# One reciprocal for a head's four chunks, and the norm's mean and epsilon inside the logarithm, in an attention kernel with two mixer blocks

## The chip, the cores and the metric

One core of a Trainium2 chip runs the kernel. The metric is device time in microseconds (us) of one execution. A profiled execution gives, beside its time, the time of every instruction on the engines: PE (TensorE: matmuls and transposes, PEld being its weight loads), DVE (VectorE), ACT (ScalarE), POOL (GpSimd) and SP (SyncE, whose queue issues the DMAs).

## The reference

Attention over 4 batches of 12 heads (448 tokens, 64 wide), with q and k normalized by their root mean square, and then two mixers over tokens and channels:

```python
def _attn_ref(q, k, v, g_q, g_k):
    def rmsnorm(x, g):
        rms = np.sqrt(np.mean(x * x, axis=-1, keepdims=True) + 1e-06)
        return x / rms * g
    q_n, k_n = (rmsnorm(q, g_q), rmsnorm(k, g_k))
    scores = (1.0 / np.sqrt(q.shape[-1])) * np.matmul(q_n, k_n.transpose(0, 1, 3, 2))
    scores = scores - np.max(scores, axis=-1, keepdims=True)
    attn = np.exp(scores)
    attn = attn / (np.sum(attn, axis=-1, keepdims=True) + 1e-09)
    return np.matmul(attn, v)
# x: (4, 448, 768) from the heads; h = ((x^T U) V)^T; u = x + h
# x = u + relu(u @ w_ch1) @ w_ch2                      w_ch1: 768 x 3072
# u = x + (relu(x^T @ w_tok1) @ w_tok2)^T
# out = u + relu(u @ w_ch1') @ w_ch2'                  w_ch1': 768 x 1536
```

## The kernel before

**Stages.** The heads are numbered 0 to 47; two neighbours make a pair, and a pair's q, k and v are loaded together. Heads 0 to 23 (batches 0 and 1) run alone at the start: the lone heads. The number 24 at which this ends is called `seam`. Heads 24 to 47 (batches 2 and 3) run beside the first mixer's channel product of batches 0 and 1 (`ffn`). Everything behind that is mixers: their weights come as 64 bit words, are converted on ACT, DVE and POOL (`to_f32`, tiles `w_bits`, lines 130 to 139), and are split in two parts each.

**A pair's norm** is `load_pair`: squares (`sq`, line 378) and their sums (`ms`, line 379), then on 16 columns the mean with epsilon (line 381), an ACT logarithm and an ACT exponential of minus half of it (lines 383, 384), and a Newton step (`nt`, lines 386 to 389) that gives the factor `rs`; q and k times `rs` are `qn` and `kn` (line 397). For pair 0 the small operations run on DVE (`first`), for all others on POOL. `turn_pair` transposes q and k on PE (`tt`), splits them in `both`, and lays them out by DMA in `qs` and `ks`.

**A head's softmax** is `softmax`: four chunks of 112 rows, and for each a score product on PE (`sc`), a negated row maximum on DVE (`nm`, line 459) and an exponential on ACT (`p`, line 461), which also leaves the row's sum in a column of `sm`. After every second chunk POOL adds 1e-9 to the two sums (line 464), DVE takes their reciprocal (line 465) and POOL scales the two chunks (line 468). A lone head's softmax stands two heads ahead of its product with v, `weigh`: transposes of the four chunks on PE (`pt`), copies on ACT and DVE (`ph`, `pl`), and products (`pv`). For the lone heads `p` has 12 buffers, three heads' worth, and the scores have three PSUM banks.

**Order.** Program text order isn't what the engines run: the framework places each engine's instructions by a simulated timeline when the program is built. Each engine then runs its own list in order, waiting at semaphores. So an edit in one place can reorder the lists elsewhere.

Of the kernel before, what the change touches and what calls it, by code (L numbers as in the profile page):

```python
# [9 lines left out]
F32 = mybir.dt.float32  # L10
# [3 lines left out]
AF = mybir.ActivationFunctionType  # L14
ALU = mybir.AluOpType
# [9 lines left out]
def attention_then_two_mixers(  # L25
# [30 lines left out]
    nc = tc.nc  # L56
    P = 128
    B, H, S, D = q.shape
    DM = out.shape[2]
    CP, NC4 = 112, 4  # L60
# [9 lines left out]
    const = ctx.enter_context(tc.tile_pool(name="const", bufs=1))  # L70
# [21 lines left out]
    for o in (0, D):  # L92
        nc.scalar.dma_start(gq2[o:o + D], g_q.rearrange("(d o) -> d o", o=1))
        nc.scalar.dma_start(gk2[o:o + D], g_k.rearrange("(d o) -> d o", o=1))
    gg = const.tile([P, 1], F32, name="gg")
    nc.vector.tensor_mul(gg, gq2, gk2)
    nc.vector.tensor_scalar_mul(gg, gg, 1.0 / D ** 0.5)
# [7 lines left out]
    pools = {"late": False, "split_u": nc.vector}  # L105
# [7 lines left out]
    def psum(kind, shape, name):  # L113
        pool = pools[kind]
        return pool.tile(shape, F32, tag=pool.name, name=name)
# [241 lines left out]
    def fetch_heads(b, hp, names):  # L357

        h0 = 2 * hp
        res = []  # L360
        for nm in names:
            t = pools["at"].tile([CP, 2, NC4, D], F32, tag="vr" if nm == "v" else "qkr", bufs=AT[nm + "r"],
                        name=f"{nm}r")
            nc.sync.dma_start(t, dict(q=q, k=k, v=v)[nm][b, h0:h0 + 2].rearrange(
                "h (p c) d -> p h c d", c=NC4))
            res.append(t)
        return res

    def load_pair(b, hp, turn, qk):
        first = turn == 0  # L370
        mul = nc.vector.tensor_mul if turn in (0, 2, 3) else nc.gpsimd.tensor_mul
        qr, kr, vr = qk + fetch_heads(b, hp, "v")

        ms = pools["at"].tile([CP, 2, 8], F32, tag="ms", name="ms")
        for i, t in enumerate((qr, kr)):
            sq = pools["at"].tile([CP, 2 * NC4, D], F32, tag="sq", bufs=AT["sq"], name="sq")
            tt = t.rearrange("p h c d -> p (h c) d")
            mul(sq, tt, tt)
            nc.vector.reduce_sum(ms[:, i], sq, axis=AX.X)
        small = nc.vector if first else nc.gpsimd  # L380
        small.tensor_scalar(ms, ms, 1.0 / D, 1e-6, op0=ALU.mult, op1=ALU.add)
        rs = pools["at"].tile([CP, 2, 8], F32, tag="rs", name="rs")
        nc.scalar.activation(rs, ms, AF.Ln)
        nc.scalar.activation(rs, rs, AF.Exp, scale=-0.5)
        nt = pools["at"].tile([CP, 2, 8], F32, tag="nt", name="nt")
        small.tensor_mul(nt, rs, rs)
        small.tensor_mul(nt, nt, ms)
        small.tensor_scalar(nt, nt, -0.5, 1.5, op0=ALU.mult, op1=ALU.add)
        small.tensor_mul(rs, rs, nt)

        def scale(i, shape):
            return rs[:, i].rearrange("p (h c) -> p h c", h=2).unsqueeze(3).to_broadcast(shape)

        qn, kn = [], []
        for i, (nm, t, n) in enumerate((("qn", qr, qn), ("kn", kr, kn))):
            n.append(pools["at"].tile([CP, NC4, 2, D], F32, tag=nm, bufs=AT["qn"], name=nm))
            mul(
                n[0].rearrange("p c h d -> p h c d"), t, scale(i, [CP, 2, NC4, D]))
        qn, kn = qn[0], kn[0]

        return qn, kn, vr
# [45 lines left out]
            res.append((qs, ks[:, 0], ks[:, 1]))  # L447
        return res

    def softmax(pr, qs, ks, kt):  # L450
        for c in range(NC4):
            if c % 2 == 0:
                sm = pools["at"].tile([CP, 2], F32, tag="sm", bufs=6, name="sm")
            sc = psum("s", [CP, S], "sc")
            cs = slice(c * CP, (c + 1) * CP)
            mm(sc, qs[:, cs], ks, True, False)
            mm(sc, qs[:, cs], kt, False, True)
            nm = pools["at"].tile([CP, 1], F32, tag="nm", bufs=8, name="nm")
            nc.vector.tensor_reduce(nm, sc, axis=AX.X, op=ALU.max, negate=True)  # L459
            p = pools["pp"].tile([CP, S], F32, tag="p", bufs=AT["p"], name="p")  # L460
            nc.scalar.activation(p, sc, AF.Exp, bias=nm, accum_out=sm[:, c % 2:c % 2 + 1])  # L461
            pr.append(p)
            if c % 2:
                nc.gpsimd.tensor_scalar_add(sm, sm, 1e-9)
                nc.vector.reciprocal(sm, sm)  # L465
                for i in range(2):
                    x = pr[c - 1 + i]
                    nc.gpsimd.tensor_scalar(x, x, sm[:, i:i + 1], 1.0, op0=ALU.mult, op1=ALU.mult)  # L468
            yield

# [42 lines left out]
    def attention(pairs, seam):  # L513
# [3 lines left out]
        n = 2 * len(pairs)  # L517
        loaded, turned, values, probs, fetched = {}, {}, {}, {}, {}
        dst = None

        def soft(h):
            if not 0 <= h < n:
                return iter(())
            probs[h] = []
            return softmax(probs[h], *turned[h // 2][h % 2])

        for t in range(-8, n):
            ahead = 2 if t < seam else 1
# [20 lines left out]
            h = due(3)  # L549
# [3 lines left out]
            h = due(7)  # L553
            if h < n:
                fetched[h // 2] = fetch_heads(*pairs[h // 2][:2], "qk")
            h = due(5)
# [632 lines left out]
```

## Time and profile before

| | |
|---|---|
| median of 3 runs | 1529.53 us (1521.19, 1529.53, 1531.46) |
| profiled execution, its own time | 1526.91 us |
| its span, first to last instruction | 1525.1 us |
| mean granted clock of TensorE | 0.985 |
| busy share of the span: PE, DVE, POOL, ACT | 94%, 77%, 59%, 49% |

The span is 1.8 us shorter than the execution's time. The busy shares are means over stages that differ much: POOL is at 59% over the whole, but at over nine tenths in parts of the first 200 us. A time in the rows below is counted from the first instruction of the span.

### The profile page before, as it was taken

What the parts mean: (1) busy time and instruction counts of PE and PEld (TensorE: products, weight loads), DVE (VectorE), ACT (ScalarE), POOL (GpSimd) and SP (SyncE); (2) the same over time, 40 slices, a digit from 0 to 9 for tenths busy, and PEclk for the clock granted to TensorE, in tenths of its full rate; (3) what the DMA queues carried; (4) which work ended last, traced back from release to release, by engine and by line L of the source; (5) the groups of instructions that cost most, each with busy time, mean ns of one, the idle gap of its engine ahead of it and who ended that gap; (6) DMA issues with size and microseconds to landing.
All of it is one profiled execution on the core that took longest, in us unless ns stands there. A gap on an engine that the chain in (4) does not pass through costs nothing.

```text
span 1525.1 us, 22086 instructions
## 1 busy us (share of the span) xinstructions
PE 1436.3 (94%) x7396; PEld 1271.5 (83%) x7396; DVE 1170.3 (77%) x1805; ACT 745.6 (49%) x1508; POOL 902.3 (59%) x943
## 2 busy tenths in 40 slices
PE   4899988999999999999999999999999999989997
PEld 3666767888888889888898998888999998979996
DVE  6888877888787788676758675477898988577886
ACT  4687755666566665444535343335343431334421
POOL 5889936777766565455655454047777755213842
PEclk9999979999999999999999999999999999999999
DMA  6676646777766565765637664355445463323343
GB/s 170 151 174 153 151 163 208 245 212 224 236 209 199 166 209 188 247 231 189 221 120 248 227 238 143 102 194 154 157 148 163 147 196 118 120 83 120 126 123 103
DMA packets 144385, 266.06 MB, mean 174 GB/s; under 512 B 12832, under 2 KB 104448, under 8 KB 144160
## 3 DMA queue, kind: packets, MB, share of 16 engines
q1 hardware_dynamic: 143952, 264.65, 55.6%
q8 instruction: 59, 0.97, 0.3%
q14 instruction: 54, 0.44, 0.1%
q10 hardware_dynamic: 320, 0.00, 0.0%
HBM read 149.72 MB, written 79.10 MB: 150 GB/s over the span
## 4 chain that ended last, share of the span: by engine, by line
PE 52%; DVE 8%; DMA 4%; POOL 3%; ACT 2%; issue 2%; SPq 0%; DVEq 0%; POOLq 0%; ACTq 0%
PE ps_x L79 23%; PE ps_p L79 10%; PE ps_g L79 10%; PE ps_t L79 2%; PE ps_u L79 2%; DVE w_bits L136 1%; DVE w_bits L131 1%; DVE w_bits L132 1%; POOL w L150 1%; PE pv L79 1%; ACT w_bits L130 1%; PE pt L487 1%; PE sc L79 1%; POOL w_bits L139 1%; DMA qs<-both 1%
## 5 line engine op out<-in xcount | busy, mean ns | idle before, releaser
L79 PE MATMUL ps_x<-gs,w 128*128 128x448 f32 x1440 | 326.0, 373 | 7.6 <-DVE gs L656 3.9
L79 PE MATMUL ps_g<-u,w 128*128 128x448 f32 x1440 | 312.7, 370 | 4.0 <-DMA w<-h_a 1.6
L79 PEld LDWEIGHTS ps_x<-gs,w 128*128 128x128 f32 x1440 | 267.9, 191 | 34.5 <-DVE gs L656 6.9
L79 PEld LDWEIGHTS ps_g<-u,w 128*128 128x128 f32 x1440 | 270.2, 189 | 27.6 <-DMA w<-h_a 1.8
L79 PE MATMUL ps_x<-gs,w_b 128*128 128x448 f32 x1026 | 226.5, 366 | 6.9 <-DVE xT L852 3.9
L139 POOL TENSOR_TENSOR w_bits<-w_bits,w_round 128x768 uint32<-128x768 uint32 (+3 forms) x80 | 145.1, 1814 | 121.0 <-DVE w_bits L136 68.9
L79 PEld LDWEIGHTS ps_x<-gs,w_b 128*128 128x128 f32 x1026 | 191.9, 188 | 24.4 <-DVE xT L852 5.0
L150 POOL TENSOR_TENSOR w<-w_bits,w 128x768 fp32r<-128x768 f32 (+3 forms) x82 | 148.1, 1816 | 82.9 <-ACT w L149 74.8
L686 DVE TENSOR_TENSOR xT<-ps_x,xT 128x448 f32<-128x448 f32 x216 | 132.2, 618 | 43.5 <-PE ps_x L79 41.2
L150 POOL TENSOR_TENSOR w_b<-w_f,w_b 128x384 fp32r<-128x384 f32 x104 | 119.0, 1157 | 68.2 <-ACT w_b L149 67.9
L468 POOL TENSOR_SCALAR p<-p,sm 112x448 f32<-112x448 f32 x192 | 131.4, 697 | 19.4 <-DVE sm L465 16.1
L79 PE MATMUL sc<-ks,qs 128*112 128x448 f32 x384 | 125.2, 412 | 18.5 <-ACT p L461 15.2
L461 ACT ACTIVATE p<-sc,nm 112x448 f32<-112x448 f32 x192 | 121.5, 635 | 37.8 <-DVE nm L459 36.4
L300 POOL TENSOR_TENSOR w_f<-w_f 128x384 f32<-128x384 f32 x26 | 29.1, 1118 | 176.1 <-DMA w_f<-c_a 99.0
L459 DVE TENSOR_REDUCE nm<-sc 112x1 f32<-112x448 f32 x192 | 116.0, 614 | 12.4 <-PE sc L79 11.9
L487 PEld LDWEIGHTS pt<-ident,p 112*112 112x112 f32 x768 | 88.6, 134 | 32.2 <-issue 9.1
L487 PE MATMUL pt<-ident,p 112*112 112x112 f32 x768 | 109.3, 260 | 3.0 <-DVE pl L502 1.9
L498 ACT ACTIVATE ph<-pt 112x448 fp32r<-112x448 f32 (+1 forms) x168 | 88.3, 545 | 38.4 <-PE pt L487 37.5
L131 DVE TENSOR_SCALAR w_bits<-w_bits 128x768 f32<-128x768 f32 (+3 forms) x80 | 65.2, 815 | 52.4 <-ACT w_bits L130 52.3
L135 ACT ACTIVATE w_round<-w_raw 128x768 uint32<-128x768 uint32 (+3 forms) x80 | 69.9, 874 | 66.4 <-POOL w_bits L139 60.0
L502 DVE TENSOR_TENSOR pl<-pt,ph 112x448 fp32r<-112x448 f32 x144 | 86.9, 615 | 18.3 <-ACT ph L498 17.8
L130 ACT ACTIVATE w_bits<-w_raw 128x768 f32<-128x768 f32 (+3 forms) x80 | 70.0, 875 | 57.5 <-POOL w L150 31.1
(141 smaller groups left out, 2718.0 us busy)
## 6 DMA issues: line engine op xcount, KB each, us to landing
w_raw<-in_moe_w_ch_dram SPq DMA_DIRECT2D x72, 768.0 KB, 5.1
w_b<-h_a SPq DMA_DIRECT2D x65, 384.0 KB, 4.3
h_a<-w SPq DMA_DIRECT2D x56, 384.0 KB, 2.7
ks<-both SPq DMA_DIRECT2D x92, 224.0 KB, 3.7
c_a<-w_bits SPq DMA_DIRECT2D x40, 384.0 KB, 4.4
w_f<-c_a SPq DMA_DIRECT2D x40, 384.0 KB, 3.1
h_b<-w SPq DMA_DIRECT2D x32, 384.0 KB, 2.5
w_b<-h_b SPq DMA_DIRECT2D x29, 384.0 KB, 3.8
```

What stands on the lines that cost most here:

```text
L79: nc.tensor.matmul(o, lhsT=l, rhs=r, start=start, stop=stop)
L130: nc.scalar.activation(f(w), f(high), AF.Abs)
L131: nc.vector.tensor_scalar_max(f(w), f(w), TINY)
L139: nc.gpsimd.tensor_tensor(w, w, r, op=ALU.add)
L150: nc.gpsimd.tensor_sub(lo, w, f(hi))
L459: nc.vector.tensor_reduce(nm, sc, axis=AX.X, op=ALU.max, negate=True)
L461: nc.scalar.activation(p, sc, AF.Exp, bias=nm, accum_out=sm[:, c % 2:c % 2 + 1])
L468: nc.gpsimd.tensor_scalar(x, x, sm[:, i:i + 1], 1.0, op0=ALU.mult, op1=ALU.mult)
L487: nc.tensor.transpose(pt[:, c * CP:(c + 1) * CP], pr[c][:, kc * CP:(kc + 1) * CP], ident[:CP, :CP],)
L498: nc.scalar.activation(ph, pt, AF.Copy)
L502: nc.vector.tensor_sub(pl, pt, f(ph))
L686: nc.vector.tensor_add(xT[:, dc], px, xT[:, dc])
```

## The change

Lone heads from the third on (`2 <= h < seam`, 22 heads) take all four sums in one tile of four columns: one addition of 1e-9, one reciprocal and then four scalings, where there were two additions, two reciprocals and twice two scalings. Heads 0, 1 and 24 to 47 keep groups of two. The tile `sm` has 4 buffers of four columns in place of 6 of two.

In the norm, the logarithm now reads the raw sum of squares, with the scale 1/64 and the epsilon as its bias from a new constant tile `eps`. The Newton step's other factor, minus half of the mean with epsilon, is one operation into `nt` that needs only `ms`, and stands beside the logarithm and not ahead of it. The square of `rs` goes into `ms`. For pair 0, on DVE, the last two operations become one. For the other pairs POOL has as many operations as before, five.

```diff
+    eps = const.tile([P, 1], F32, name="eps")
+    nc.vector.memset(eps, 1e-6)
...
         small = nc.vector if first else nc.gpsimd
-        small.tensor_scalar(ms, ms, 1.0 / D, 1e-6, op0=ALU.mult, op1=ALU.add)
+        nt = pools["at"].tile([CP, 2, 8], F32, tag="nt", name="nt")
         rs = pools["at"].tile([CP, 2, 8], F32, tag="rs", name="rs")
-        nc.scalar.activation(rs, ms, AF.Ln)
+        nc.scalar.activation(rs, ms, AF.Ln, scale=1.0 / D, bias=eps[:CP])
+        small.tensor_scalar(nt, ms, -0.5 / D, -0.5e-6, op0=ALU.mult, op1=ALU.add)
         nc.scalar.activation(rs, rs, AF.Exp, scale=-0.5)
-        nt = pools["at"].tile([CP, 2, 8], F32, tag="nt", name="nt")
-        small.tensor_mul(nt, rs, rs)
+        small.tensor_mul(ms, rs, rs)
         small.tensor_mul(nt, nt, ms)
-        small.tensor_scalar(nt, nt, -0.5, 1.5, op0=ALU.mult, op1=ALU.add)
-        small.tensor_mul(rs, rs, nt)
+        if first:
+            small.scalar_tensor_tensor(rs, nt, 1.5, rs, op0=ALU.add, op1=ALU.mult)
+        else:
+            small.tensor_scalar_add(nt, nt, 1.5)
+            small.tensor_mul(rs, rs, nt)
...
-    def softmax(pr, qs, ks, kt):
+    def softmax(pr, n, qs, ks, kt):
         for c in range(NC4):
-            if c % 2 == 0:
-                sm = pools["at"].tile([CP, 2], F32, tag="sm", bufs=6, name="sm")
+            if c % n == 0:
+                sm = pools["at"].tile([CP, NC4], F32, tag="sm", bufs=4, name="sm")[:, :n]
...
-            nc.scalar.activation(p, sc, AF.Exp, bias=nm, accum_out=sm[:, c % 2:c % 2 + 1])
+            nc.scalar.activation(p, sc, AF.Exp, bias=nm, accum_out=sm[:, c % n:c % n + 1])
             pr.append(p)
-            if c % 2:
+            if c % n == n - 1:
                 nc.gpsimd.tensor_scalar_add(sm, sm, 1e-9)
                 nc.vector.reciprocal(sm, sm)
-                for i in range(2):
-                    x = pr[c - 1 + i]
+                for i in range(n):
+                    x = pr[c + 1 - n + i]
                     nc.gpsimd.tensor_scalar(x, x, sm[:, i:i + 1], 1.0, op0=ALU.mult, op1=ALU.mult)
...
-            return softmax(probs[h], *turned[h // 2][h % 2])
+            return softmax(probs[h], NC4 if 2 <= h < seam else 2, *turned[h // 2][h % 2])
```

Where this puts the instructions: over the program DVE has 22 fewer, POOL 22 fewer, and PE, ACT and SP as many as before. Lines of the changed kernel count 2 more from the norm on and 5 more behind it (the scaling is its line 473, the addition 469). Each engine's list is in another order up to the end of the attention; behind that it is the same list.

On POOL, before, from the scaling of head 17 to that of head 18, among the later lone heads (`vs` is the split of v, `sq` the squares of a later pair):

```order
L468 TENSOR_SCALAR p<-p,sm 112x448 x2
L464 TENSOR_SCALAR sm<-sm 112x2
L386 TENSOR_TENSOR nt<-rs 112x16
L468 TENSOR_SCALAR p<-p,sm 112x448 x2
L150 TENSOR_TENSOR vs<-vr,vs 112x4x64
L387 TENSOR_TENSOR nt<-nt,ms 112x16
L464 TENSOR_SCALAR sm<-sm 112x2
L378 TENSOR_TENSOR sq<-kr 112x512
L468 TENSOR_SCALAR p<-p,sm 112x448 x2
L388 TENSOR_SCALAR nt<-nt 112x16
L464 TENSOR_SCALAR sm<-sm 112x2
L468 TENSOR_SCALAR p<-p,sm 112x448 x2
```

On POOL, in the changed kernel, the scaling of head 18 with what stands ahead of it:

```order
L469 TENSOR_SCALAR sm<-sm 112x4
L152 TENSOR_TENSOR vs<-vr,vs 112x4x64
L386 TENSOR_SCALAR nt<-ms 112x16
L380 TENSOR_TENSOR sq<-qr 112x512
L394 TENSOR_TENSOR rs<-rs,nt 112x16
L473 TENSOR_SCALAR p<-p,sm 112x448 x4
```

One addition of four columns stands where there were two of two, with four other operations between it and the four scalings, which now stand in one run.

On DVE, before, the norm of pair 0 at the start of the program:

```order
L381 TENSOR_SCALAR ms<-ms 112x16
L96 TENSOR_TENSOR gg<-gq_72,gk_73 128x1
L97 TENSOR_SCALAR gg<-gg 128x1
L386 TENSOR_TENSOR nt<-rs 112x16
L387 TENSOR_TENSOR nt<-nt,ms 112x16
L388 TENSOR_SCALAR nt<-nt 112x16
L379 TENSOR_REDUCE ms<-sq 112x8
L389 TENSOR_TENSOR rs<-rs,nt 112x16
L397 TENSOR_TENSOR qn<-qr,rs 112x2x4x64
```

On DVE, in the changed kernel, the same place:

```order
L386 TENSOR_SCALAR nt<-ms 112x16
L98 TENSOR_TENSOR gg<-gq_72,gk_73 128x1
L99 TENSOR_SCALAR gg<-gg 128x1
L388 TENSOR_TENSOR ms<-rs 112x16
L389 TENSOR_TENSOR nt<-nt,ms 112x16
L391 SCALAR_TENSOR_TENSOR rs<-nt,rs 112x16
L381 TENSOR_REDUCE ms<-sq 112x8
L402 TENSOR_TENSOR qn<-qr,rs 112x2x4x64
```

The product of the two gains (`gg`, which waits for their DMAs) still stands ahead of the Newton step; the factor `rs` is ready one operation and one reduction earlier in the list, and the scaling of q keeps its place behind the reduction.

## Rows read from the trace of the kernel before

**Rows 1.** The page of the whole execution: span, and each engine's busy us.

```profile
span 1525.1 us, 22086 instructions
...
PE 1436.3 (94%) x7396; PEld 1271.5 (83%) x7396; DVE 1170.3 (77%) x1805; ACT 745.6 (49%) x1508; POOL 902.3 (59%) x943
```

**Rows 2.** Busy us of each engine in stretches; PEclk is the granted clock.

```profile
core 0: us, PE busy (x) PEld busy (x) DVE busy (x) ACT busy (x) POOL busy (x), PEclk, DMA share, GB/s
...
45.00:100.00 55.00, 49.66 (x284) 37.46 (x283) 46.27 (x97) 40.06 (x111) 45.74 (x87) 0.97 0.63 152
100.00:133.00 33.00, 28.46 (x158) 19.95 (x157) 30.86 (x64) 25.12 (x68) 30.97 (x55) 1.00 0.65 160
133.00:188.00 55.00, 53.15 (x317) 39.79 (x316) 47.47 (x99) 43.94 (x119) 51.68 (x99) 1.00 0.64 157
...
196.00:240.00 44.00, 36.64 (x154) 29.26 (x154) 35.10 (x59) 26.10 (x48) 16.75 (x12) 0.81 0.50 169
240.00:300.00 60.00, 54.22 (x286) 47.40 (x286) 47.08 (x83) 35.53 (x77) 46.46 (x53) 0.97 0.74 225
```

**Rows 3.** Lines of POOL's additions (L464), from 45, 100 and 133 us on.

```profile
L464 POOL TENSOR_SCALAR sm<-sm 112x2 f32<-112x2 f32 x15 | 3.2, 214 | 4.3 <-ACT p L461 3.3
...
L464 POOL TENSOR_SCALAR sm<-sm 112x2 f32<-112x2 f32 x10 | 2.1, 214 | 0.9
...
L464 POOL TENSOR_SCALAR sm<-sm 112x2 f32<-112x2 f32 x16 | 3.4, 214 | 1.4
```

**Rows 4.** Timeline of POOL, 172 to 176 us.

```profile
172.06 0.21 POOL L464 TENSOR_SCALAR sm<-sm 112x2 f32<-112x2 f32 x1
172.35 0.20 POOL L381 TENSOR_SCALAR ms<-ms 112x16 f32<-112x16 f32 x1
...
175.01 0.21 POOL L464 TENSOR_SCALAR sm<-sm 112x2 f32<-112x2 f32 x1
175.32 1.26 POOL L468 TENSOR_SCALAR p<-p,sm 112x448 f32<-112x448 f32 x2
```

**Rows 5.** Timeline: end of head 13's last exponential (ACT), its first scaling (POOL).

```profile
115.45 0.24 ACT L461 ACTIVATION_READ_ACCUMULATOR p<-sc,nm 112x1 f32 x1
...
122.83 1.26 POOL L468 TENSOR_SCALAR p<-p,sm 112x448 f32<-112x448 f32 x2
```

**Rows 6.** Timeline of PE, 122 to 124 us.

```profile
122.15 0.91 PE L79 MATMUL pv<-ph,vr 112*128 112x448 f32 x2
122.55 0.71 PE L79 MATMUL pv<-pl,vs 112*128 112x448 f32 x1
123.10 0.55 PE L487 MATMUL pt<-ident,p 112*112 112x112 f32 x4
123.42 0.64 PE L79 MATMUL sc<-ks,qs 128*112 128x448 f32 x2
```

**Rows 7.** Timeline of the start: norms of pairs 0 and 2.

```profile
8.22 0.17 DVE L387 TENSOR_TENSOR nt<-nt,ms 112x16 f32<-112x16 f32 x1
8.43 0.17 DVE L388 TENSOR_SCALAR nt<-nt 112x16 f32<-112x16 f32 x1
...
17.39 0.69 DVE L379 TENSOR_REDUCE ms<-sq 112x8 f32<-112x512 f32 x1
...
18.24 0.20 POOL L381 TENSOR_SCALAR ms<-ms 112x16 f32<-112x16 f32 x1
```

**Rows 8.** Lines of ACT and DVE, 100 to 196 us.

```profile
L465 DVE RECIPROCAL sm<-sm 112x2 f32<-112x2 f32 x26 | 4.0, 156 | 1.3 <-POOL sm L464 1.1
L429 ACT ACTIVATE both<-tt 128x448 fp32r<-128x448 f32 x7 | 3.9, 559 | 0.6 <-PE tt L418 0.4 <-DMA ks<-both 0.2
L425 ACT ACTIVATE both<-tt,gg 128x448 fp32r<-128x448 f32 x6 | 3.8, 637 | 3.6 <-issue 1.6 <-DMA ks<-both 1.1 <-DMA qs<-both 0.9
```

**Rows 9.** Waits from 200 to 615 us: engine, waited for, total, times, longest.

```profile
POOL sm L464 <- ACT p L461: 32.0, 26, 4.6
...
PE sc L79 <- ACT p L461: 8.5, 7, 2.4
```

## The prediction

> **What bounds the kernel now.** I read the page first, then the time by stretches, then in the stretch that the change touches the lines of POOL and its timeline, and last the waits.
>
> The page gives PE 1436.3 us of a span of 1525.1 [rows 1], so over the whole program PE is the engine that is hardly ever without work. The change removes nothing from PE. It can pay only where PE waits, and only in the first 200 us, since that is where lone heads run. The stretches show how much there is to win [rows 2] (the columns are the stretch, its length, then the busy time of PE, PEld, DVE, ACT and POOL). From 45 to 100 us PE is busy 49.66 of 55, so it idles 5.3; from 100 to 133 it idles 4.5; from 133 to 188 only 1.85. POOL idles 9.3, 2.0 and 3.3 there. DVE is nearly as full, 30.86 of 33 in the second stretch. The lone heads thus have no engine that is alone the bound. POOL and DVE are the tightest in the second stretch, PE in the third.
>
> That PE's 1.85 us are real in the third kind of stretch is to be read from starts, since matmuls overlap: at 122.15 a product, at 122.55 the next, at 123.10 four transposes, at 123.42 score products [rows 6]. Each starts before the one ahead has ended. PE is handed work there as fast as it takes it.
>
> A rule speaks against this reading. The Trainium skill ("Perfetto Trace Analysis", section "Identifying the Most-Contended Engine") holds matmul busy time to be a poor measure of how full TensorE is, because pipelined matmuls mislead, and would have weight-load busy time used. Weight loads are busy 39.79 of the 55 us [rows 2], so by that page PE would have 15 us to spare and the whole of POOL's saving would come through; the time it gives is a rival below.
>
> POOL's place is seen in one head. The last of head 13's four exponentials is done at 115.69 (115.45 and 0.24), and POOL comes to the head's first scaling at 122.83 [rows 5]: 7.1 us later, with its own list in between. A scaling waits for POOL's list, not for exponentials.
>
> **The change part by part.**
>
> The removed additions on POOL. An addition at 172.06 is followed by POOL's next operation at 172.35, one at 175.01 by the next at 175.32 [rows 4]: 0.30 each, nearly all of it fixed. The trace has no addition of four columns; an operation of POOL on 16 columns takes 0.20, as long as one on two (0.21) [rows 4], so I take the same 0.30. Half of the additions in each stretch go [rows 3].
> - 45 to 100 us: 15 additions, 7.5 of them go, 2.2 us. POOL idles 9.3 here, 4.3 of it right ahead of additions, 3.3 for exponentials [rows 2, 3], so some of the saving becomes idle time. I take half, 1.1; the bounds are 0 and 2.2.
> - 100 to 133 us: 10, so 5 go, 1.5 us. POOL is full, and PE has 4.5 us to take it up. I take 1.5.
> - 133 to 188 us: 16, so 8 go, 2.4 us. PE can gain no more than its 1.85 us of idle time. I take half of that, 0.9; the bounds are 0 and 2.4, the upper if PE isn't full after all.
>
> Sum 3.5 us. The first 45 us hold only the first few heads, two of which keep their groups, and the pipeline is filling there; I take nothing.
>
> The removed reciprocals on DVE: 22 of 0.156 [rows 8], 3.4 us. They lie beside other work, except that in the second stretch DVE is as full as POOL; that the 1.5 us above come through there needs this relief too. I count no more for it. If it hid nothing, the saving on POOL in that stretch would stop at DVE's 2.1 idle us, which is still over 1.5.
>
> The added wait. The first two chunks' scalings now wait for the fourth exponential. What covers this is the 7.1 us that POOL is late [rows 5], and that POOL idles only 0.9 and 1.4 us ahead of its additions in the two later stretches, none of it listed as a wait for ACT [rows 3]. I take 0. If the cover were gone, the whole list of POOL behind the addition would wait: scalings of the head before, the norm, `qn` and `kn`, and with them PE's `tt`. That is a rival.
>
> The norm. For pair 0 one operation of DVE goes: 8.22 to 8.43, 0.21 [rows 7]. The start of the logarithm comes earlier by as much, but the Newton step stands behind `gg` in DVE's list as before. For the other pairs a hop over POOL goes from the path: pair 2's sums end on DVE at 18.08 (17.39 and 0.69), and POOL starts the mean only at 18.24 and ends it at 18.44 [rows 7], 0.36 that ACT need not wait. While the pipeline fills this is on the path, later `load_pair` is pairs ahead of its use. I take 0.5 for both, with bounds 0 and 1.
>
> ACT's logarithm gets its bias from a tile. The nearest rows: the copy with a scale from a tile (`gg`) takes 637 ns, the one without 559 [rows 8], so 0.08 each, 2 us for 24, half of it in the lone stage. ACT is busy 43.94 of 55 where it is fullest [rows 2], so this hides; 0, at worst 1. The Trainium skill ("ScalarE: Activation LUTs", section "What ACT_TABLE_LOAD costs") puts each such operand at about 93 ns, an estimate of 2.2 us for 24 by its figure; the trace agrees within 0.02 each, and the sum stays as it is.
>
> The order from 196 us to the end of the attention. Nothing is removed there, but every list is permuted locally. I take 0, with a width from what waits there: PE idles 7.4 us from 196 to 240 (at a granted clock of 0.81, so between 1.2 and 2.4 GHz) and 5.8 to 300 [rows 2], 13 us that a better order could win at most; it waits 8.5 us in 7 pieces for a score bank [rows 9], and as much again is what I give a worse one. Behind the attention the lists are the same, so what was won or lost is passed on.
>
> Sum: 3.5 + 0.5 = 4.0 us. Against the profiled execution, 1526.9 - 4.0 = 1522.9. That execution lies 2.6 below the median of three; the mean of all four is 1527.3, and from it I forecast 1527.3 - 4.0 = **1523.3 us**. A measurement of this kernel can tell about 1% from no change, 15 us: under 1512 is faster, over 1542.6 slower.
>
> **The rivals.**
> - *PE was the bound in the lone stage.* POOL's and DVE's freed time becomes idle time. For it: PE's unbroken starts [rows 6]. Against it: 9.8 us of idle PE from 45 to 133. Time: 1527.3.
> - *POOL alone sets the pace.* All bounds at once, 2.2 + 1.5 + 2.4 + 1.0 = 7.1: 1520.2. For it: POOL's 7 us of lateness. This is what the page on weight loads would have, and the starts in [rows 6] speak against it in the longest stretch.
> - *The addition stalls POOL* (slower). If POOL comes to a lone head's addition before the fourth exponential is done, its list stands. Beside the mixer this is so already: 26 waits, 32.0 us, 1.23 each [rows 9]. At that price 22 heads cost 27 us: 1523.3 + 27 = 1550. It decides where POOL's lateness falls under the time of two exponentials; a saving of 0.3 a head doesn't use up 7 us.
> - *A new order beside the mixer.* Well placed, 13 us more: 1510.3. Badly, 8.5: 1531.8.
>
> **How the numbers follow.** Forecast 0.40, PE the bound 0.22, POOL alone 0.12, stalls of POOL 0.08, a better order 0.10, a worse one 0.08. The last two have no better ground than that local moves of up to some tens of matmuls can fall either way. Faster by over 1% is the better order, 0.10; slower is the stalls, 0.08; the rest, 0.82, is within 1%. The range goes from about the better order's end, 1511, to past the worse one's, 1537, where the runs' own spread of some 5 us to either side is added; it leaves out the stalls and half of the better order.
>
> **What would show it.** In the changed kernel POOL should have 74 additions, no more idle time ahead of those of the lone heads than now, and the lone stage's last heads should end some 4 us earlier, PE's idle time from 45 to 188 us being smaller by about that. Waits of POOL for exponentials in the lone stage would show the stall; an unmoved end of the stage would show PE as the bound; a stage that ends earlier and a mixer that doesn't would show the order. The forecast fails if the second stage moves by more than the first can give.

## The result, and the profile after

The changed kernel takes **1537.71 us** (median of 10 runs, 1534.92 to 1541.00), the kernel before 1528.74 (10 runs, 1521.19 to 1533.47). The ratio of the two, taken over their runs, is 1.0072, with a 95% interval of 1.0049 to 1.0095: slower by 9 us going by the medians, by 11 going by the ratio. The forecast was 1523.3, its range ended at 1537. The change went the other way than forecast. A worse order was among the rivals, but it was looked for in the wrong place, beside the mixer.

The page of the changed kernel, span and busy us of each engine (`...` marks lines left out, here and below):

```profile
span 1534.2 us, 22056 instructions
...
PE 1444.4 (94%) x7396; PEld 1273.9 (83%) x7396; DVE 1177.9 (77%) x1783; ACT 747.5 (49%) x1508; POOL 903.9 (59%) x921
```

Against [rows 1], POOL and DVE have 22 instructions fewer each, as they should, and the span is 9.1 us longer. To see where, I followed one landmark through both traces: the last operation on each lone head, DVE's `xT`. For head 23, the last of the lone heads, that operation in the trace of before and in that of after is

```profile
195.37 0.62 DVE L511 TENSOR_TENSOR xT<-pv,tmp 64x448 f32<-64x448 f32 x1
```

```profile
202.95 0.62 DVE L516 TENSOR_TENSOR xT<-pv,tmp 64x448 f32<-64x448 f32 x1 [0.20 <-ACT tmp L515]
```

so the lone stage ends 7.6 us later (203.57 for 195.99). Read the same way, head 5 ends 3.0 us earlier than before (80.4 for 83.3), head 8 4.2 earlier (98.8 for 103.0), head 11 2.2 earlier, head 14 0.8 later, head 20 3.7 later. By 100 us the changed kernel is ahead, by more than the 1.6 us that were forecast for there, and then 11.8 us are lost between 99 and 204 us. Behind that hardly anything changes: a step of the first mixer that stands at 617.5 us before, near the attention's end (an ACT copy into `gs`), is 9.0 us late, and the end of the program 9.1.

The stretches of [rows 2] in the changed kernel, with the same columns:

```profile
45.00:100.00 55.00, 49.72 (x281) 36.75 (x280) 46.37 (x90) 41.72 (x116) 49.40 (x90) 0.97 0.58 154
100.00:133.00 33.00, 30.60 (x175) 22.33 (x174) 29.18 (x59) 26.65 (x73) 28.85 (x49) 0.99 0.65 167
133.00:188.00 55.00, 49.72 (x269) 36.53 (x266) 42.83 (x82) 37.89 (x104) 42.93 (x76) 0.94 0.56 138
...
196.00:240.00 44.00, 33.06 (x144) 25.18 (x144) 33.75 (x56) 25.10 (x47) 16.46 (x14) 0.84 0.47 159
```

The third stretch had been the one in which PE never stopped, 53.15 of 55 us; now PE, DVE, ACT and POOL all do less in it than before, and even the DMA moves less (138 GB/s for 157). When every engine idles more, none of them has become the bound; they wait for each other, or for something else.

One column more has changed, the granted clock of TensorE (PEclk): 0.94 in the third stretch, where it was 1.00. By 3 us:

```profile
139.00:142.00 3.00, 1.62 (x6) 0.91 (x7) 1.84 (x3) 2.95 (x9) 2.84 (x6) 0.89 0.01 3
142.00:145.00 3.00, 3.00 (x13) 2.31 (x12) 2.06 (x4) 1.33 (x6) 2.56 (x3) 0.54 0.33 96
145.00:148.00 3.00, 3.00 (x22) 2.48 (x21) 2.91 (x6) 2.48 (x7) 0.44 (x2) 1.00 0.93 202
...
169.00:172.00 3.00, 1.22 (x5) 0.82 (x5) 1.86 (x4) 2.53 (x8) 0.41 (x2) 1.00 0.01 4
172.00:175.00 3.00, 3.00 (x11) 2.42 (x10) 2.68 (x6) 2.29 (x7) 3.00 (x5) 0.51 0.61 156
175.00:178.00 3.00, 3.00 (x21) 2.56 (x20) 2.67 (x6) 1.97 (x5) 2.83 (x6) 0.92 0.20 43
```

Twice, behind 3 us in which PE was busy only 1.62 and 1.22, the clock is mostly at the lower of its two levels (1.2 and 2.4 GHz), and PE does 13 and 11 matmuls in 3 us where it does 22 and 21 in the next. From the means, 0.94 and 1.00 of 55 us, I estimate the loss at 3.3 us at most. It is a second cost behind the waits.

The lines of ACT and DVE from 100 to 196 us, which answer to [rows 8], say what is waited for (the last column is the idle time ahead and what ended it):

```profile
L431 DVE SCALAR_TENSOR_TENSOR both<-tt,gg,both 128x448 fp32r<-128x448 f32 x6 | 4.1, 684 | 6.7 <-ACT both L430 6.7
...
L430 ACT ACTIVATE both<-tt,gg 128x448 fp32r<-128x448 f32 x6 | 3.8, 634 | 9.7 <-DMA qs<-both 8.6 <-issue 1.1
```

ACT's copy of a pair's transposed q into `both` waits 8.6 us for DMAs `qs<-both`, where it had waited 0.9. `both` has one buffer for q and one for k, so the copy for the next pair's q can't start before the four layout DMAs `qs` of the pair ahead have read it. What stands behind the copy in ACT's list waits too. Two such places in ACT's timeline, and PE's at the first (the bracket is the idle time ahead):

```profile
138.97 0.63 ACT L430 ACTIVATE both<-tt,gg 128x448 fp32r<-128x448 f32 x1 [2.97 <-DMA qs<-both]
...
169.47 0.63 ACT L430 ACTIVATE both<-tt,gg 128x448 fp32r<-128x448 f32 x1 [3.44 <-DMA qs<-both]
```

```profile
140.38 0.60 PE L423 MATMUL tt<-ident,kn 112*128 112x112 f32 x4 [2.25 <-DVE both L431]
```

The chain of waits in the same stretch runs through these DMAs; they are its largest single pieces there (start, length):

```profile
134.03 4.92 DMA qs<-both
138.97 0.64 ACT both L430
139.64 0.69 DVE both L431
140.38 0.60 PE tt L423 x4
...
163.91 5.45 DMA qs<-both
```

Between the two places, from 148.32 to 160.91 us, the chain runs along POOL's list.

Why do they land late? SP's timeline ahead of the second place:

```profile
159.25 1.10 SPq L446 DMA_DIRECT2D ks<-both  x2
160.44 0.54 SPq L366 DMA_DIRECT2D kr<-in_k_dram  x1
161.07 0.91 SPq L366 DMA_DIRECT2D qr<-in_q_dram  x1
162.07 0.47 SPq L446 DMA_DIRECT2D ks<-both  x1
162.59 0.59 SPq L447 DMA_DIRECT2D qs<-both  x1
163.23 0.64 SPq L446 DMA_DIRECT2D ks<-both  x1
163.91 1.66 SPq L447 DMA_DIRECT2D qs<-both  x1
```

Two input loads of later pairs (224 KB each) stand in the middle of pair 11's layout. It takes 13.5 us from its first issue to its last landing (155.91 to 169.37), and 11.2 (149.35 to 160.58) in a run below that has the old order, where these loads stand behind it.

Not every pair's layout is longer. From first issue to last landing, the layouts of pairs 7 to 12 take 14.3, 11.6, 13.2, 10.2, 13.5 and 11.8 us in the changed kernel, and 12.0, 11.8, 13.8, 12.0, 11.2 and 11.7 in that run. Pairs 7 and 11 are longer, and pairs 9 and 10, which have loads inside too, are not. Ahead of the first place shown, the load `kr` had landed at 133.59, and the next `ks` was issued at 132.25, as soon as the last score product of head 16 had freed its buffer (132.22): no load holds the layout up there. What grows there is the time between layouts: pair 10's starts 4.6 us behind the landing of pair 9's (143.59 and 138.95), in the old order 1.4. And pair 11's starts 2.1 us behind the landing of pair 10's, in the old order 0.9 ahead of it; there all four of pair 10's `qs` stand ahead of its `ks`, and ACT's copy for pair 11 doesn't wait.

SP's list for pairs 8 to 11, read from the two programs (K and Q are layout DMAs with the number of their pair, kr, qr and v are loads with theirs):

```diff
-Q8 Q8 v8 K8 K8 K8 Q8 K8 Q8 kr11 qr12 Q9 Q9 v9 K9 K9 K9 Q9 K9 Q9 kr12 qr13 v10 Q10 Q10 kr13 Q10 Q10 qr14 K10 K10 K10 K10 Q11 Q11 v11 K11 K11 K11 Q11 K11 Q11 kr14 qr15
+qr11 Q8 kr11 v8 Q8 K8 K8 K8 Q8 K8 Q8 qr12 v9 Q9 Q9 K9 K9 kr12 K9 Q9 K9 Q9 qr13 kr13 v10 Q10 Q10 K10 K10 qr14 K10 Q10 K10 Q10 Q11 Q11 v11 K11 K11 kr14 qr15 K11 Q11 K11 Q11
```

In the old order too, two loads stand inside one layout, pair 10's. So the theory to test: **the change moved the lists, the new order puts loads into the layouts, and the late layouts hold up ACT.** The rival: **the grouping itself costs,** the addition or the scalings waiting for the fourth exponential. The trace gives the rival little: POOL's additions from 133 to 188 us,

```profile
L469 POOL TENSOR_SCALAR sm<-sm 112x4 f32<-112x4 f32 x7 | 1.6, 222 | 3.0 <-ACT p L466 2.6
```

wait 2.6 us for exponentials, where [rows 3] had none in that stretch. That isn't 11.8, but waits can hide behind each other, so it was tried.

### The profile page after: what moved, and what is told of

It is laid out like the page before. It is cut to its first block, busy times and chain, and to the rows that moved or that the text cites. A ratio compares the mean times of both kernels' runs of the same rounds, so it can differ in the third digit from the quotient of the medians.

```text
span 1534.2 us, 22056 instructions
## 1 busy us (share of the span) xinstructions
PE 1444.4 (94%) x7396; PEld 1273.9 (83%) x7396; DVE 1177.9 (77%) x1783; ACT 747.5 (49%) x1508; POOL 903.9 (59%) x921
## 4 chain that ended last, share of the span: by engine, by line
PE 57%; DVE 13%; DMA 9%; POOL 9%; ACT 5%; issue 5%; SPq 2%; ACTq 0%; DVEq 0%; POOLq 0%
PE ps_x L79 24%; PE ps_g L79 11%; PE ps_p L79 10%; DMA qs<-both 4%; POOL w L152 3%; PE pv L79 3%; PE sc L79 2%; DVE w_bits L133 2%; POOL w_bits L141 2%; PE pt L492 2%; DVE w_bits L138 2%; PE ps_t L79 2%; PE ps_u L79 2%; DVE w_bits L134 1%; ACT w_bits L132 1%
## 5 line engine op out<-in xcount | busy, mean ns | idle before, releaser
L464 DVE TENSOR_REDUCE nm<-sc 112x1 f32<-112x448 f32 x192 | 116.8, 613 | 15.0 <-PE sc L79 14.0
L133 DVE TENSOR_SCALAR w_bits<-w_bits 128x768 f32<-128x768 f32 (+3 forms) x80 | 76.1, 952 | 63.1 <-ACT w_bits L132 63.1
L507 DVE TENSOR_TENSOR pl<-pt,ph 112x448 fp32r<-112x448 f32 x144 | 87.5, 615 | 11.6 <-ACT ph L503 11.3
```

Of the source, the lines that this page charges most:

```text
L133: nc.vector.tensor_scalar_max(f(w), f(w), TINY)
L507: nc.vector.tensor_sub(pl, pt, f(ph))
```

## The experiments

To part the operations from their order, a kernel can carry a table that fixes each engine's list. It adds edges without semaphores between neighbours in the wanted order, so that nothing but the order changes:

```diff
+def pin(tc):     # ORDER: per engine, the traced positions in the wanted order
+    ...
+        for a, b in zip(at, at[1:]):
+            tc.add_manual_dep(
+                mine[b], mine[a].name,
+                mybir.DependencyInfo(mybir.DependencyClass.NoSync, mybir.DependencyReason.DATA),
+                reason="pinned order")
...
         attention_then_two_mixers(tc, *args)
+        pin(tc)
```

Times are given with the ratio to the kernel before on the same chip, and with the end of head 23 in the profile (196.0 before, 203.6 after), which is that of one execution.

**Operations against order.** *New operations, old order*: the changed kernel with the table of the kernel before (the removed operations dropped, a head's four scalings together at the place of its third).

```diff
 # open lists of the changed kernel
+ORDER = (lists of the kernel before)
```

> The changed kernel's operations, with each engine's list pinned to that of the kernel before (the removed operations left out; a lone head's four scalings stand where the last two stood). Theory O, the new order of the lists costs the time and the removed operations gain what was forecast: 1528.7 - 4 = about 1525, at most 1529. Theory G, the grouping itself costs it (scalings that wait for the fourth exponential, POOL's list behind them): as slow as the changed kernel, about 1537.

Measured: 1524.55 us, ratio 0.9997 (0.9979 to 1.0016), head 23 at 192.8. In the old order the grouping of four has no net cost.

*Old operations, new order*: the kernel before with the table of the changed kernel.

```diff
 # lists of the kernel before
+ORDER = (lists of the changed kernel)
```

> The operations of the kernel before, with each engine's list pinned to that of the changed kernel (the two additions and the two reciprocals of a lone head stand side by side in the place of the one). Theory O: as slow as the changed kernel or slower by the operations that are back, 1538 to 1542. Theory G, the four-wide operations cost the time: about 1529. In this order the first two scalings stand behind the fourth exponential too, so if this kernel is slow and the pinned changed one also, it is the place of the scalings.

Measured: 1557.78 us, ratio 1.0215 (1.0194 to 1.0236), head 23 at 220.6. The new order alone makes the kernel before 33 us slower, and more than the changed kernel is slower by. Why it is so much worse with the old operations I didn't follow; the granted clock is lower there too, 0.90 from 100 to 133 us and 0.89 to 188.

**Halves of the change,** without a table, each in the order that it gets by itself.

```diff
-            return softmax(probs[h], *turned[h // 2][h % 2])
+            return softmax(probs[h], NC4 if 2 <= h < seam else 2, *turned[h // 2][h % 2])
 # the sums in fours alone; the norm as before
```

> The softmax part of the change alone, lists as the framework orders them. Theory G: about 1537, since the grouping is all in it. Theory O: a third order of the lists, so a time of its own, anywhere from 1520 to 1540, not bound to the changed kernel's.

Measured: 1545.22 us, ratio 1.0126 (1.0102 to 1.0151), head 23 at 200.0; and the mixer's step at 617.5 us is 11.1 late.

```diff
-        nc.scalar.activation(rs, ms, AF.Ln)
+        nc.scalar.activation(rs, ms, AF.Ln, scale=1.0 / D, bias=eps[:CP])
 # the norm's edit alone; the sums in twos as before
```

> The norm part of the change alone, lists as the framework orders them. Theory G: about 1528, within 1 us of before, as nothing is grouped and the norm removes one operation. Theory O: this small edit too moves some 600 DVE and 190 POOL operations, so it should move the time by several us, either way, though it removes next to nothing.

Measured: 1530.78 us, ratio 1.0041 (1.0021 to 1.0060), head 23 at 191.6 and the step at 617.5 us 1.1 earlier than before. So small an edit reorders hundreds of instructions too: at least 384 on DVE and 144 on POOL stand elsewhere. The profile's attention is not slower, and the loss in the timed runs isn't explained by it; that stays open. Behind the step at 617.5 us this profile takes 916.8 us, and that of the kernel before 907.6, with the same lists there; the control below takes 916.2 at a ratio of 1.0000. So the end of a single profile says little about a few us. The two halves add up to 1.7% and the whole is 0.7%: they are not terms of a sum, each has an order of its own.

**A control, and the place in time.** *Old operations, old order*: the kernel before with its own table.

```diff
 # lists of the kernel before
+ORDER = (the same lists)
```

> The kernel before with its own five lists written out as a fixed table. A control: all theories say ratio 0.998 to 1.002 against the kernel before. Its profile is one of the kernel before from the same chip and hour as the others. If the removed additions and the shorter norm are worth 3 to 4 us in the lone stage, head 8 ends near 103 and head 23 near 196 us in it, against 99.9 and 192.8 in the run of the new operations in the old order; if they are worth nothing, it ends these within 1 us of that run.

Measured: 1530.25 us, ratio 1.0000 (0.9972 to 1.0028): the table by itself costs nothing. Head 8 ends at 101.3 and head 23 at 194.4, between the two expectations. Two profiles of the same lists thus differ by 1.6 us there, all of it by head 5; the granted clock from 45 to 100 us is 0.97 in the one [rows 2] and 1.00 in the control.

*New order from 100 to 204 us alone*: what the changed kernel starts in that time, in its order, and the old order ahead and behind.

```diff
-ORDER = (lists of the kernel before)
+ORDER = (old lists to 100 us, new lists to 204 us, old lists)
```

> The new operations; all five lists are in the old order, but for what the changed kernel starts between 100 and 204 us, which is in the new order. If the loss sits in the lists of the later lone heads: head 23 ends 7 to 11 us later than with the old order throughout (200 to 204 us, not 192.8), and the time is 1531 to 1536 us against 1525 or so of the old order. If the loss needs what the new order does ahead of 100 us or behind 204 us: head 23 within 2 us of 192.8 and the time within 3 us of the old order's.

Measured: 1537.88 us, ratio 1.0059 (1.0036 to 1.0081), the whole loss in the timed runs. The profile is of the fastest of its four executions (1530.24; the others took 1535.71 to 1540.85). In it head 8 ends at 96.9 and head 23 at 197.7, between the two expectations: from one to the other it takes 100.8 us, where the old order with the same operations takes 92.5 to 92.9 and the changed kernel 104.8. ACT waits as in the changed kernel, but the clock stays at 1.00:

```profile
ACT both L430 <- DMA qs<-both: 8.2, 4, 3.1
```

```profile
133.00:188.00 55.00, 49.32 (x284) 35.55 (x283) 43.34 (x82) 39.56 (x106) 44.89 (x81) 1.00 0.58 143
```

So the waits come with this order, and the 4.0 us more of the changed kernel's profile are about what its lower clock was estimated at, as far as one profile of each can tell.

**SP's list against the others.** *Loads inside the layouts*: the old order on all engines, but SP has the changed kernel's list for pairs 7 to 13.

```diff
 SP, pair 9 and what stands beside it
-Q9 Q9 v9 K9 K9 K9 Q9 K9 Q9 kr12 qr13
+v9 Q9 Q9 K9 K9 kr12 K9 Q9 K9 Q9 qr13
```

> The new operations in the old order, but SP's list for pairs 7 to 13 is that of the changed kernel (loads of q and k inside the layouts). If the place of the loads costs the time: ACT waits for qs 6 us or more between 100 and 204 us, head 23 ends at 198 us or later and not 192.8, the time is 1530 to 1535 us. If the other engines' order is the cause: head 23 within 2 us of 192.8, time within 3 us of the old order's 1525 or so.

Measured: 1540.69 us, ratio 1.0083 (1.0049 to 1.0118), head 23 at 205.0. Moving a few DMAs within one engine's list is as dear as the whole change, and dearer than the 1535 us that were expected at most. The waits from 100 to 204 us, and SP's timeline at pair 9:

```profile
ACT both L430 <- DMA qs<-both: 15.3, 5, 5.5
PEld sc L79 <- ACT p L466: 12.9, 6, 5.0
```

```profile
128.37 1.10 SPq L447 DMA_DIRECT2D qs<-both  x2
130.88 1.10 SPq L446 DMA_DIRECT2D ks<-both  x2
137.91 0.32 SPq L366 DMA_DIRECT2D kr<-in_k_dram  x1
138.32 0.46 SPq L446 DMA_DIRECT2D ks<-both  x1
```

Here the load costs still more than its transfer: SP stands from 131.98 to 137.91 at `kr`, whose buffer POOL frees with a `qn` that ends at 137.88. The next `ks` needs a buffer that the score products of head 16 had freed at 134.84; it waits 3.1 us more behind the load. Such waits are long here. SP's own at loads, from 100 to 204 us:

```profile
SPq L366 <- POOL qn L402: 24.6, 7, 5.8
```

In the changed kernel this line has 2.4 us. So the run shows what SP's list alone can cost, and not that the changed kernel loses its time in the same way.

*Loads behind the layouts*: the changed kernel's lists, with each such load moved behind its layout on SP.

```diff
 SP, pair 9 and what stands beside it
-v9 Q9 Q9 K9 K9 kr12 K9 Q9 K9 Q9 qr13
+v9 Q9 Q9 K9 K9 K9 Q9 K9 Q9 kr12 qr13
```

> The changed kernel's own lists, but on SP from pair 5 on each load of q or k that stands inside a pair's eight layout DMAs stands right behind the last of them. If the loads inside the layouts delay the layouts, and these the copies of the next pair: the waits of ACT for qs fall from 8.6 us (100 to 204 us) to under 3, head 23 ends at 194 to 198 us and not 203.6, and the time is 1526 to 1531 us. If the order on the other engines is what costs, and the layouts are late because their own copies are: head 23 at 201 us or later, time 1534 us or more. Slower than the changed kernel would mean that the loads themselves are needed there in time.

Measured: 1560.05 us, ratio 1.0195 (1.0173 to 1.0217), head 23 at 219.7. The waits for `qs` fall to 1.7 us as expected, and the kernel gets slower by some 20 us more. I had expected a repair; the last sentence of the expectation is what happened. The waits from 100 to 204 us:

```profile
POOL sq L380 <- DMA kr<-in_k_dram: 19.3, 4, 7.7
PEld pt L492 <- POOL p L473: 16.8, 9, 5.0
```

POOL stands at the squares of k until the load lands, its scalings queue behind, and PE's transposes wait for these. In the new order POOL needs the load earlier. Read from the lists of the changed kernel and of the new operations in the old order, the number of scalings (four a head) that stand ahead of the squares of q and k:

```
pair                 10  11  12  13  14  15
sq of q, old order   44  52  60  68  76  84
sq of q, new order   40  48  56  68  72  80
sq of k, old order   48  56  68  72  80  88
sq of k, new order   44  52  60  68  80  84
```

For most of these pairs POOL's norm has moved ahead by a head's four scalings.

*All lists new but SP's*, from 100 to 204 us, the other half of the two by two:

```diff
-ORDER = (old to 100 us, new to 204 us, old), all engines
+ORDER = the same, but SP in the old order throughout
```

> The new operations; from 100 to 204 us PE, DVE, ACT and POOL have the new order, SP keeps the old one (the other half of the two by two with the loads inside the layouts on SP alone). The new list of POOL has the squares of later pairs up to one head ahead of their old place. If it is SP's list alone that costs, head 23 ends within 3 us of 192.8 and the time is 1525 to 1529 us. If each list fits only the other one (loads early for squares that stand early), POOL waits 10 us or more for kr, head 23 ends at 205 us or later, and the time is 1538 us or more, as with the loads moved behind the layouts.

Measured: 1546.17 us, ratio 1.0122 (1.0094 to 1.0151), head 23 at 214.0, and POOL again at the loads:

```profile
POOL sq L380 <- DMA kr<-in_k_dram: 17.8, 4, 5.8
```

Head 23 thus ends at 191.5 to 192.8 with all lists old, 205.0 with SP's new, 214.0 with all but SP's new, and 197.7 (203.6 in the changed kernel) with all new. The whole new order costs less than either part of it. My reading, which no run isolates, is that its early loads fit its early squares.

The clock goes with it. From 100 to 133 and from 133 to 188 us the granted clock is 1.00 and 1.00 in the kernel before, in the old order with either operations, with the new order from 100 us and in both runs with half loads below, and head 23 ends at 191 to 198 us in all of these. It is 0.99 and 0.94 in the changed kernel, 0.95 and 0.94 with SP's list new, 0.83 and 0.91 with all but SP's new, 0.87 and 0.88 with the loads behind the layouts, and 0.90 and 0.89 with the old operations in the new order, where head 23 ends at 204 to 221. Of the halves of the change, the sums alone have their lower clock ahead of that, 0.94 from 45 to 100 us. By these means, an estimate, the clock is worth up to 4 us in the changed kernel and 5 to 11 in the other four; the rest goes with the waits.

**The loads' bytes.** *Half loads*: the changed kernel in its order; from pair 9 on only the first head's q and k of a pair are loaded, and the second head is computed from them.

```diff
+            m = 1 if nm != "v" and 6 * b + hp >= 9 else 2
-            nc.sync.dma_start(t, dict(q=q, k=k, v=v)[nm][b, h0:h0 + 2].rearrange(
+            nc.sync.dma_start(t[:, :m], dict(q=q, k=k, v=v)[nm][b, h0:h0 + m].rearrange(
                 "h (p c) d -> p h c d", c=NC4))
-            res.append(t)
+            res.append(t if m == 2 else t[:, :1].to_broadcast([CP, 2, NC4, D]))
```

> The changed kernel in its own order, but from pair 9 on only the first head of a pair's q and k is loaded (half the bytes of each load; the second head is computed from the first one's data). If the loads' own transfers delay the layouts behind them: the waits of ACT for qs from 100 to 204 us fall from 8.6 to 5 us or less, head 23 ends at 197 to 201 us and not 203.6, time 1528 to 1534 us. If the layouts are late for another reason (their own copies, or SP standing at a load whose buffer is not free): head 23 within 1.5 us of 203.6 and the waits stay at 7 us or more.

Measured: 1532.29 us, ratio 1.0037 (1.0017 to 1.0057), head 23 at 196.9, 6.7 us earlier than in the changed kernel. The wait of ACT and the third stretch:

```profile
ACT both L430 <- DMA qs<-both: 5.0, 4, 2.1
```

```profile
133.00:188.00 55.00, 51.39 (x294) 37.06 (x293) 44.22 (x83) 39.98 (x107) 46.90 (x83) 1.00 0.53 128
```

Not all of the 6.7 us are the bytes. The clock is at 1.00 here, and the run with whole loads, the same lists from 100 us and this clock takes 100.8 us from head 8 to head 23, against 100.2 with half loads. What the bytes show by themselves is at pair 11: its layout takes 11.3 us, with whole loads 13.1 in that run and 13.5 in the changed kernel, ACT's wait behind it is 1.3 us for 3.1 and 3.4, and from the end of head 17 to that of head 18 it takes 4.8 us for 6.7 and 7.0. So they are worth some 2 us at that place. POOL's wait for `kr` from 100 to 204 us is shorter as well, 1.8 us for 2.4 and 4.3, and the run doesn't part the two.

*The same in the old order*, as a control:

```diff
 # the same edit
+ORDER = (lists of the kernel before)
```

> The same halved loads with the new operations in the old order, as a control. If loads cost only where they stand inside a pair's layout, head 23 ends within 1.5 us of the same kernel with whole loads (192.8) and the time is within 3 us of it. If the bytes of the loads matter wherever they stand, head 23 gains 3 us or more here too.

Measured: head 23 at 191.4, against 191.5 with whole loads in the run below: where the loads stand behind the layouts (all but two of them, pair 10's), their bytes cost the lone stage nothing. The time is 1518.73 us, ratio 0.9937 (0.9913 to 0.9960), 4.6 us under that run and so outside what I expected; the profiles part between 192 us and the end of the attention, beside the mixer, which I didn't follow further; there two profiles of one program differ too (420.8 and 425.6 us from head 23 to the step at 617.5 us, in the first experiment and in the one below).

*New operations, old order, once more*, on the same chip:

```diff
+ORDER = (lists of the kernel before), as in the first experiment
```

> The new operations in the old order once more, on the chip of the three others. If the removed operations are worth the 3.5 us of the sum, the ratio is 0.9965 to 0.9985; if they are worth 1 to 2.5 us, as the two profiles in the old order have it (192.8 against 194.4 us for head 23), 0.9983 to 0.9995; if nothing, 0.9995 to 1.001. The profile should repeat head 23 at 192 to 194 us.

Measured: 1523.36 us, ratio 0.9977 (0.9958 to 0.9996), head 23 at 191.5. Of the versions that leave nothing out it is the fastest: with the first measurement, 0.9997, it is worth some 2 us over the kernel before, at the edge of what can be told. Its three stretches of the lone heads:

```profile
45.00:100.00 55.00, 50.66 (x299) 38.02 (x297) 48.30 (x94) 42.64 (x120) 47.31 (x84) 1.00 0.64 163
100.00:133.00 33.00, 29.07 (x163) 20.74 (x162) 29.73 (x60) 26.03 (x71) 30.98 (x53) 1.00 0.63 155
133.00:188.00 55.00, 52.68 (x316) 39.77 (x314) 45.91 (x88) 42.85 (x111) 48.74 (x85) 1.00 0.62 158
```

Not tried: the new order on POOL alone, or on SP and POOL alone, in that stretch. So the shares of the lists of PE, DVE and ACT in the loss are not told apart.

## Why the prediction was wrong

**The step that failed is the order.** The prediction took "the order from 196 us to the end of the attention", gave it 0 with a width of 13 and 8.5 us, and took nothing for the order of the lists in the lone stage, though every list is another from the program's start to the end of the attention. It costed what the edit removes there and treated where the rest stands as given. Measured, the order costs 11 to 15 us (the changed kernel against the new operations in the old order: 1.0072 against 0.9977 and 0.9997), in the profiles all of it between 99 and 204 us. Beside the mixer, where I had looked, nothing shows: from head 23 to the step at 617.5 us it takes 422.9 us, before 421.5, and two profiles of one program differ by 4.9 there. In the new order the norm of most later pairs stands a head or more earlier on POOL, the loads with it on SP; ACT's copies wait 8.6 us for layouts, of which those of pairs 7 and 11 are longer and pair 10's starts later; and behind two of the waits the clock falls. That the order costs this is shown by pinning it; which of the moves costs how much stays open, and why the framework's timeline sets it so I didn't follow. The prediction read POOL's list and its waits, left SP's list out, and took no change of the clock in the lone stage.

**The added wait** was taken as 0. In the old order that is right for POOL, which waits 0.5 and 0.4 us for exponentials at its additions from 100 to 204 us, and with 192.8 and 191.5 for head 23 the four chunks have no net cost. In the new order POOL waits 2.6 us for exponentials in the lone stage, two times. The rival of 27 us of stalls is thus a tenth of its size in the lone stage. Beside the mixer such waits are 31.0 us in 19 pieces, where [rows 9] had 32.0 in 26:

```profile
POOL sm L469 <- ACT p L466: 31.0, 19, 4.0
```

**The sum of the removed operations** (3.5 + 0.5) is somewhat high, with 2 to 3 us where it can be seen alone, in the old order. Head 23 ends at 192.8 and 191.5 with the new operations, at 196.0 and 194.4 with the old: 3.05 us on the mean of two. By parts, from the same four profiles and in the order new, new, old, old: from head 2 to head 8 43.6, 43.1, 46.0 and 44.6 us, 1.9 gained (1.1 was forecast for 45 to 100 us; against 44.6 alone, the one of the two with the full clock, it is 1.2); from head 8 to head 11 21.6, 21.2, 22.4 and 22.4, 0.95 gained (1.5); from head 11 to head 23 71.2, 71.2, 70.6 and 70.7, 0.55 lost (0.9 gained). The 0.75 that is gained up to head 2 (0.5 for the norm) can't be told from chance: two further runs with the old lists up to 100 us end head 0 at 40.8 and 41.0 us and not at 44 to 45. So the additions were worth about what was forecast at first, less in the second stretch and nothing in the last. My reading is that PE was the bound there, as the rival had it: POOL's busy time from 133 to 188 us falls from [rows 2]'s 51.68 to 48.74, PE's is 52.68 for 53.15, and the relief becomes idle time. It isn't shown against one other: PE waits more for exponentials at its score products there, 4.1 and 3.5 us from 100 to 204 us with the new operations in the old order, 1.2 and 1.8 with the old ones, and this can be a price of the grouping. Of the 3 us some 2 are seen in the medians, with an uncertainty as large. The rival by which POOL alone would set the pace (7.1 us) falls. By the Trainium skill ("Perfetto Trace Analysis", section "Identifying the Most-Contended Engine"), which goes by weight loads and by the matmuls' share of the peak, PE had 15 us to spare in that stretch, as far as weight loads tell; it took up none of POOL's 2.9. The starts in [rows 6] spoke for a full PE too, but they are from 122 to 124 us, in the stretch where the prediction counts 4.5 us of idle PE, and so no evidence for the last one.

**The bias from a tile** was put at 0.08 us each. ACT's logarithms, before and after:

```profile
L383 ACT ACTIVATE rs<-ms 112x16 f32<-112x16 f32 x24 | 5.2, 218 | 15.0 <-POOL ms L381 9.8 <-DVE ms L381 4.5 <-POOL kn L397 0.6
```

```profile
L385 ACT ACTIVATE rs<-ms,eps 112x16 f32<-112x16 f32 x24 | 7.4, 309 | 7.3 <-DVE ms L381 6.6 <-POOL kn L402 0.7
```

They take 91 ns more each, 2.2 us in all. The Trainium skill's page "ScalarE: Activation LUTs" (section "What ACT_TABLE_LOAD costs") gives 93 ns for such an operand, and this row agrees. The hop over POOL is gone from the idle time ahead, as forecast.

**The width** was too small for what it stood for. An order that nobody has timed is worth more than any term of the sum here: the runs with one order or another lie between 0.9977 and 1.0215.

## What to carry to other kernels

Where a framework orders the engines' lists by its own timeline, an edit is two changes, the operations and a new order, and the second can be the larger: look at the list of every engine in the stretch that is edited, the DMA queue's first, not only behind it. Compare which transfers stand ahead of those that someone waits for, and which consumers have moved ahead of their loads. To know what the operations are worth, pin the old order and time them in it; if there is a gain, ship it so. And read the granted clock in every stretch: a wait that leaves PE idle can cost again in the clock behind it.

## What the runs showed of the hardware

Loads of 224 KB that are issued among layout DMAs on the same queue can delay them: in the new order halving the loads took 2.2 us off pair 11's layout (13.5 to 11.3) and brought ACT's waits from 8.6 to 5.0 us; in the old order it gained the lone stage nothing. The DMA was only 56% busy from 133 to 188 us, but full where the loads and the layout met, so the mean doesn't tell (the last two columns are its share and GB/s):

```profile
161.00:163.00 2.00, 1.92 (x13) 1.40 (x12) 1.83 (x5) 2.00 (x7) 1.70 (x3) 1.00 0.90 201
163.00:166.00 3.00, 3.00 (x18) 2.27 (x17) 1.67 (x4) 2.10 (x6) 1.82 (x3) 1.00 1.02 286
```

At the second of the two places nothing overtook the load: `kr`, issued at 160.44, landed at 166.11, 5.7 us later, `ks`, issued behind it at 162.07, at 168.30, 6.2 us later, where half of all `ks` from 100 to 204 us land within 3.4. The Trainium skill ("DMA: Bandwidth & Descriptors", section "Queues, rings and completion order") has each DMA engine take descriptors in ring order, and these times agree. A load whose buffer isn't free holds the issuing engine and all that stands behind it, 3.1 us in the place shown. TensorE's granted clock fell to 0.54 and 0.51 behind 3 us in which PE was busy 1.62 and 1.22, and PE's matmuls in 3 us fell to about half. And such lists are sensitive: the same few loads a few places earlier cost 12 us in one order (192.8 to 205.0), and a few places later 16 in another (203.6 to 219.7).
